# One batch of attention over each MLP, a pipelined head, and squares and value casts on GpSimd, in a fused attention and mixer kernel

## The chip, the cores and the metric

One core of one Trainium2 chip (trn2). The time is that of the device for one execution, in microseconds. Most executions of one kernel agree within 0.3%. Every run was timed beside the kernel before on the same chip, and results were compared with the reference. An execution is called slow here when it took over 1.5% longer than the fastest of the same kernel.

## The reference, cut to what matters

```python
batch, n_heads, seq, head_dim = 8, 12, 448, 64        # d_model = 768, rank = 32
def attn(q, k, v, g_q, g_k):                           # q, k, v: [8, 12, 448, 64] float32
    q_n, k_n = rmsnorm(q, g_q), rmsnorm(k, g_k)        # over head_dim, eps 1e-6
    scores = q_n @ k_n.T / sqrt(64)
    return softmax(scores) @ v
def mixer(x, U, V, w_ch1, w_ch2):                      # x: [8, 448, 768], from attn
    u = x + (x.T @ U @ V).T                            # low-rank mix along seq
    return u + relu(u @ w_ch1) @ w_ch2                 # 768 -> 3072 -> 768
```

The MLP has the most arithmetic. Attention needs TensorE too, but also ScalarE (exponentials) and VectorE (norms, copies out of PSUM, divisions), so both kernels weave pieces of attention between pieces of an MLP.

## The kernel before

Words used throughout: a *tile* `t` is four heads of one batch (three tiles per batch), loaded together. A *pair* `p` is two heads, half a tile (six pairs per batch). Per pair TensorE makes 8 transposes (to `pt`), 8 score matmuls (to `sc`) and 32 value matmuls (to `o`). `pt` and `o` share one PSUM buffer, the pool `ps_o`. The *head* is everything up to the first matmul of the first MLP (`ph`); *after the head* is the rest. One MLP has 24 groups of `ph` matmuls, then the `po` matmuls. An even batch uses 384 columns and an odd one 512, because a seventh of every even batch (64 of its 448 columns) is carried into the odd one.

The parts that the change and the argument touch, with cuts marked:

```python
def setup():                                  # (cut)
    for half in range(2):
        nc.scalar.dma_start(gg[...], g_q...); nc.scalar.dma_start(gk2[...], g_k...)
    nc.vector.tensor_mul(gg, gg, gk2)         # first work of VectorE: waits for g
def setup_mix():
    nc.gpsimd.memset(Uf, 0.0)
    for ...:                                  # 14 small loads
        nc.scalar.dma_start(Uf[...], Ur[j, p0:p1, :])
    nc.vector.tensor_copy(Ub, Uf)
    for i in range(4):
        nc.scalar.dma_start(Vf[...], moe_V)
    nc.vector.tensor_copy(V4..., Vf...)       # (cut)
def load(t):                                  # SyncE's queue, qk has 2 buffers
    nc.sync.dma_start(qk[:, 0], q[...]); nc.sync.dma_start(qk[:, 1], k[...])
def load_v(t):                                # GpSimd's queue; the DMA casts to bf16
    for h in range(HG):
        nc.gpsimd.dma_start(va[:, h, :, 0:D], v[b, h0 + h]...)
def stats(t):
    for s in range(2):
        nc.scalar.activation(sq[:, s], qk[:, s], AF.Square)
        nc.vector.tensor_reduce(rstd[:, s]..., sq[:, s]..., AX, OP.add)
    nc.scalar.activation(rs, rs, AF.Ln, bias=eps); nc.scalar.activation(rs, rs, AF.Exp, scale=-0.5)
def scale(t):                                 # four tensor_tensor: qkn = qk * rstd
    ...
def transposes(p):                            # pt from ps_o, then
    nc.vector.tensor_scalar(qT, pt[:, 0], gg, None, OP.mult); nc.vector.tensor_copy(kT, pt[:, 1])
def values(p, hh):                            # o from ps_o, then three VectorE operations
    ...
def attention(b):                             # order within a pair
    for p in range(b * 6, b * 6 + 6):         # scores(p, (0, 1)), expo(p, 0)
        ...                                   # values(p - 1, 0); expo(p, 1)
        ...                                   # even pair: stats(t + 1)
        ...                                   # scores(p, (2, 3)), expo(p, 2)
        ...                                   # values(p - 1, 1); expo(p, 3)
        ...                                   # odd pair: scale(t + 1), load(t + 3)
        ...                                   # transposes(p + 1)
# the order of work
attention(0) ; setup_mix() in the middle of it
for b in range(B):
    if b == 0:
        for _, piece in first[:6] + mixing(0): piece()      # first = attention(1)
        weave(fill, 24 * 384, first[6:])                    # 11 pairs over the first MLP
        weave(fill, total - 24 * 384 - 3000, attention(2))
    else:
        weave(fill, total * 0.84, attention(b + 2) or the last two values)
    weave(fill, total * 0.13, mixing(b + 1))
```

## Time and profile before

| | before |
|---|---|
| time, median of 4 | 719.97 us (719.29 to 720.61) |
| span in the profile | 719.2 us |
| head (up to the first `ph` matmul) | 89.25 us |
| after the head | 629.97 us |
| TensorE idle in the head / after it | 50.95 / 34.03 us |

Idle times in these tables are sums of the gaps in front of TensorE's matmuls in the trace. From the page of the kernel before: the share of time in which TensorE was busy, then its busy tenths in 40 slices of 18 us, and the clock that it was granted:

```profile
PE 629.4 (88%) x5168; PEld 357.1 (50%) x5168; DVE 342.7 (48%) x773; ACT 272.0 (38%) x385; POOL 80.4 (11%) x126
...
PE   1606787878899999989999999989999999999997
...
PEclk9999799989999999999999999999999999999999
```

The kernel is bound by TensorE, with a slow head. By stretch (columns: the stretch, its length, busy time and count for each engine, the granted clock, the share of the DMA engines and GB/s); these are the head, the first three MLPs with what is woven into them, and the last MLP, which carries nothing:

```profile
core 0: us, PE busy (x) PEld busy (x) DVE busy (x) ACT busy (x) POOL busy (x), PEclk, DMA share, GB/s
0.00:89.25 89.25, 38.20 (x342) 23.02 (x343) 38.86 (x92) 36.62 (x48) 29.75 (x54) 0.94 1.05 169
89.25:199.70 110.45, 89.02 (x868) 51.40 (x869) 64.51 (x153) 55.85 (x77) 15.47 (x22) 0.95 0.50 85
199.70:284.80 85.10, 83.38 (x675) 45.63 (x673) 45.11 (x101) 34.31 (x48) 8.45 (x12) 1.00 0.33 60
284.80:356.70 71.90, 68.38 (x623) 40.53 (x621) 40.06 (x92) 32.92 (x48) 8.44 (x12) 1.00 0.36 65
650.30:719.20 68.90, 64.06 (x349) 33.73 (x346) 13.66 (x22) 7.17 (x12) 0.00 (x0) 1.00 0.10 29
```

TensorE is busy for 38 of the 89 us of the head. The first MLP, which carries 11 pairs, takes 110 us and leaves 21 us idle. Its even successor, with six pairs, takes 72 us. The busy time of the last line stops short of 68.9 us because the last store is in it.

Why the head is slow shows in the timeline (start, length, engine, line, operation, output and input, count; in brackets the idle time of the engine before it and what ended it):

```profile
10.80 0.16 DVE L100 TENSOR_TENSOR gg<-gg,gk_93 128x1 f32<-128x1 f32 x1 [10.80 <-DMA gk_93<-in_g_k_dram]
10.88 2.34 DVE L155 TENSOR_REDUCE rstd<-sq 112x16 f32<-112x1024 f32 x2
...
39.09 9.06 ACTq L112 DMA_DIRECT2D Uf<-in_moe_U_dram  x13
...
51.37 0.29 DVE L113 CAST Ub<-Uf 128x256 bf16<-128x256 f32 x1 [12.53 <-DMA Vf<-in_moe_V_dram]
...
54.62 0.99 PE L194 MATMUL sc<-qT,kT 64*112 64x448 bf16 x4 [14.79 <-DVE kT L185]
...
57.61 1.06 PE L215 MATMUL o<-va_98,E_95 112*128 112x65 bf16 x16
```

The first reduce stands behind the gain multiply, and that waits for `g` until 10.8 us, although the first squares were done at 5.9 us. Then 14 loads of U and 4 of V leave ScalarE's queue for 12.7 us. VectorE's copy of U stands in front of the copies of the next transposes, so TensorE waits 14.79 us. The last line gives 1.06 us for 16 value matmuls. Later in the trace the same group takes 0.67 us:

```profile
94.33 0.67 PE L215 MATMUL o<-va_97,E_95 112*128 112x65 bf16 x16
```

Eight transposes take 1.16 us in the head and 0.57 us later. So TensorE runs the head at about half speed. The row PEclk reads 9 there because the trace's clock records begin only at 74.4 us; the durations show it.

What TensorE waited for after the head (who, for whom: us in all, times, longest):

```profile
PE sc L194 <- DVE kT L185: 13.3, 19, 1.5
...
PE pt L180 <- DVE xs_100 L222: 6.7, 5, 2.1
PE pt L180 <- DVE qkn L168: 6.6, 16, 1.4
...
PE pt L180 <- DVE xs_101 L222: 4.5, 3, 1.9
```

Scores wait for the copy of `kT` out of PSUM, and transposes for `qkn`, the output of `scale`, and for `ps_o` to be evicted. All of it is VectorE's work, and 21.5 of the 34 us are in the first MLP. Squares and `scale` on the same page (busy us, mean ns, then the idle before them):

```profile
L168 DVE TENSOR_TENSOR qkn<-qk,rstd 112x512 bf16<-112x512 f32 x96 | 59.7, 682 | 1.0 <-ACT rstd L159 0.7
...
L154 ACT ACTIVATE sq<-qk 112x1024 f32<-112x1024 f32 x48 | 48.2, 1058 | 4.0 <-DMA qk<-in_q_dram 2.9
```

### The profile page before, as it was taken

How to read it: one execution, taken by the hardware profiler on the slowest of the kernel's cores; microseconds unless marked ns; L12 is line 12 of the kernel's file. 1: busy time of each engine (PE TensorE's matmuls, PEld its weight loads, DVE VectorE, ACT ScalarE, POOL GpSimd, SP SyncE). 2: the span in 40 equal slices, each digit the busy share in tenths (PEclk: the TensorE clock that was granted, in tenths of full speed). 3: DMA queues.
4: the chain of work that ended last, by engine and by line, in shares of the span. 5: the costliest groups of instructions: out<-in, count | busy, mean ns of one | idle time of the engine just before them, and what ended most of it. 6: DMA issues, size and time to landing. Idle time of an engine off the chain costs nothing.

```text
span 719.2 us, 12074 instructions
## 1 busy us (share of the span) xinstructions
PE 629.4 (88%) x5168; PEld 357.1 (50%) x5168; DVE 342.7 (48%) x773; ACT 272.0 (38%) x385; POOL 80.4 (11%) x126
## 2 busy tenths in 40 slices
PE   1606787878899999989999999989999999999997
PEld 0303444444454565555554556555544656664464
DVE  3425655656555545645556544654555333233211
ACT  2615455555354530664165322554255211101200
POOL 7203111112001010111010110111000000000000
PEclk9999799989999999999999999999999999999999
DMA  9995993345413333234413423324300010010011
GB/s 143 221 174 83 224 147 59 49 71 102 83 29 62 48 69 92 20 62 86 100 11 62 83 43 89 62 18 88 94 5 1 23 46 22 1 46 22 1 45 44
DMA packets 80854, 49.09 MB, mean 68 GB/s; under 512 B 47905, under 2 KB 77217, under 8 KB 80801
## 3 DMA queue, kind: packets, MB, share of 16 engines
q0 software_dynamic: 52416, 14.95, 20.4%
q1 hardware_dynamic: 26752, 33.04, 17.2%
q8 instruction: 40, 0.66, 0.4%
q10 hardware_dynamic: 1632, 0.35, 0.3%
q14 instruction: 14, 0.11, 0.1%
HBM read 52.25 MB, written 11.01 MB: 88 GB/s over the span
## 4 chain that ended last, share of the span: by engine, by line
PE 71%; DVE 17%; ACT 5%; DMA 4%; issue 2%; ACTq 0%; SPq 0%; DVEq 0%
PE po L296 28%; PE ph L276 24%; DVE qkn L168 7%; PE sc L194 6%; PE o L215 6%; DVE rstd L155 5%; ACT E_95 L199 2%; PE pt L180 2%; DMA qk<-in_k_dram 2%; ACT sq L154 2%; DVE qT L184 1%; PE pu L256 1%; PE pu L253 1%; PE po L294 1%; DMA gk_93<-in_g_k_dram 1%
## 5 line engine op out<-in xcount | busy, mean ns | idle before, releaser
L296 PE MATMUL po<-w2b,hT 128*128 128x384 bf16 x1344 | 246.1, 328 | 0.0
L296 PEld LDWEIGHTS <-hT 128*128 128x128 bf16 x1344 | 125.8, 98 | 81.9 <-issue 9.5
L276 PEld LDWEIGHTS <-w1b 128*128 128x128 bf16 x1152 | 104.8, 98 | 99.6 <-issue 14.1
L279 ACT ACTIVATE hT<-ph 128x384 bf16<-128x384 f32 (+1 forms) x96 | 52.2, 544 | 230.8 <-PE ph L276 230.6
L276 PE MATMUL ph<-uB,w1b 128*128 128x512 bf16 x576 | 133.4, 379 | 0.0
L199 ACT ACTIVATE E_95<-sc 112x896 bf16<-112x896 f32 x96 | 84.8, 911 | 78.2 <-PE sc L194 66.2
L281 DVE TENSOR_SCALAR hT<-ph 128x384 bf16<-128x384 f32 (+1 forms) x96 | 59.8, 623 | 101.1 <-PE ph L276 100.7
L199 ACT ACTIVATE E_96<-sc 112x896 bf16<-112x896 f32 x96 | 84.8, 914 | 51.8 <-PE sc L194 51.8
L276 PE MATMUL ph<-uA,w1b 128*128 128x384 bf16 x576 | 104.0, 326 | 0.1
L194 PE MATMUL sc<-qT,kT 64*112 64x448 bf16 x384 | 66.0, 410 | 40.3 <-DVE kT L185 34.3
L218 DVE RECIPROCAL rec<-o 128x4 f32<-128x4 f32 x96 | 17.3, 180 | 109.2 <-PE o L215 109.2
L180 PE MATMUL pt<-ident,qkn 112*128 112x112 bf16 x384 | 31.5, 224 | 42.1 <-DVE qkn L168 25.7
L155 DVE TENSOR_REDUCE rstd<-sq 112x16 f32<-112x1024 f32 x48 | 56.3, 1213 | 22.2 <-ACT sq L154 21.9
L168 DVE TENSOR_TENSOR qkn<-qk,rstd 112x512 bf16<-112x512 f32 x96 | 59.7, 682 | 1.0 <-ACT rstd L159 0.7
L194 PEld LDWEIGHTS <-kT 64*112 64x112 bf16 x384 | 21.9, 134 | 74.9 <-DVE kT L185 50.2
L180 PEld LDWEIGHTS <-qkn 112*128 112x128 bf16 x384 | 23.1, 102 | 56.8 <-DVE qkn L168 32.4
L154 ACT ACTIVATE sq<-qk 112x1024 f32<-112x1024 f32 x48 | 48.2, 1058 | 4.0 <-DMA qk<-in_q_dram 2.9
L147 POOL DMA_DIRECT2D va_99<-in_v_dram x32 | 22.5, 704 | 177.2 <-PE o L215 170.8
L215 PEld LDWEIGHTS <-E_95 112*128 112x128 bf16 x768 | 33.1, 103 | 10.4 <-issue 3.2
L215 PEld LDWEIGHTS <-E_96 112*128 112x128 bf16 x768 | 32.7, 103 | 10.8 <-issue 3.6
L147 POOL DMA_DIRECT2D va_98<-in_v_dram x32 | 22.5, 704 | 134.4 <-PE o L215 134.4
L147 POOL DMA_DIRECT2D va_97<-in_v_dram x32 | 22.6, 708 | 132.4 <-PE o L215 128.6
(99 smaller groups left out, 370.6 us busy)
## 6 DMA issues: line engine op xcount, KB each, us to landing
qk<-in_q_dram SPq DMA_DIRECT2D x24, 448.0 KB, 4.1
qk<-in_k_dram SPq DMA_DIRECT2D x24, 448.0 KB, 5.5
w1b<-in_moe_w_ch_dram POOLq DMA_DIRECT2D x6, 768.0 KB, 17.8
w2b<-in_moe_w_ch_dram POOLq DMA_DIRECT2D x6, 768.0 KB, 17.2
out_dram<-osb SPq DMA_DIRECT2D x8, 336.0 KB, 2.8
out_dram<-osb SPq DMA_DIRECT2D x8, 288.0 KB, 2.7
out_dram<-osb SPq DMA_DIRECT2D x8, 240.0 KB, 2.6
va_97<-in_v_dram POOLq DMA_DIRECT2D x32, 56.0 KB, 2.6
```

The costliest lines, as they stand in the source:

```text
L147: nc.gpsimd.dma_start(va[:, h, :, 0:D], v[b, h0 + h].rearrange("(p j) d -> p j d", j=NJ))
L154: nc.scalar.activation(sq[:, s], qk[:, s], AF.Square)
L155: nc.vector.tensor_reduce(rstd[:, s].rearrange("p h j -> p (h j)"), sq[:, s].rearrange("p h (j d) -> p (h j) d", d=D), AX, OP.add)
L168: nc.vector.tensor_tensor(qkn[:, pr, s].rearrange("p j h d -> p h j d"), qk[:, s, hp].rearrange("p h (j d) -> p h j d", d=D), rstd[:, s, h ...
L180: nc.tensor.transpose(pt[:, s, j * SP:(j + 1) * SP], qkn[:, p % 2, s, j].rearrange("p h d -> p (h d)"), ident[:SP, :SP])
L194: nc.tensor.matmul(sc[:, hh, 0:S], kT[pp, kc * SP:(kc + 1) * SP], qT[pp, :], start=True, stop=True)
L199: nc.scalar.activation(Es[p % NE][:, :, PAD + kc * S:PAD + (kc + 1) * S], scs.pop((p, kc))[:, :, 0:S], AF.Exp, scale=float(D) ** 0.5)
L215: nc.tensor.matmul(o[:, i, :], E[:, hh, c:c + P], va[:, hl, kc, :], start=(kc == 0), stop=(kc == NJ - 1))
L276: nc.tensor.matmul(ph, w1b[:, dc, hc * P:(hc + 1) * P], u[:, dc, :], start=(dc == 0), stop=(dc == KD - 1))
L279: nc.scalar.activation(hT[:, hc, 0:n], ph, AF.Relu)
L281: nc.vector.tensor_relu(hT[:, hc, 0:n], ph)
L296: nc.tensor.matmul(po, hT[:, hc, i * P:(i + 1) * P], w2b[:, hc, hs], start=False, stop=(hc == KH - 1))
```

## The change

The intent: attention is always one batch ahead and spread evenly over the whole MLP; the head is a software pipeline by pairs; squares and the casts of the values move to GpSimd; TensorE is kept warm by 30 matmuls on zeros at the start. The core of the diff, cuts marked with `...`:

```diff
-    xpool = ctx.enter_context(tc.tile_pool(name="xpool", bufs=3))
+    xpool = ctx.enter_context(tc.tile_pool(name="xpool", bufs=2))
-    NE, NV = 2, 3
+    NE, NV, NWARM, NFILL = 2, 3, 30, 0
...
-                    nc.scalar.dma_start(Uf[r:r + p1 - p0, par, i, :], Ur[j, p0:p1, :])
+                    nc.sync.dma_start(Uf[r:r + p1 - p0, par, i, :], Ur[j, p0:p1, :])
...  (loads of U and V in load_mix, called early; the copies in setup_mix, called later)
     def load_v(t):
-        for h in range(HG):
-            nc.gpsimd.dma_start(va[:, h, :, 0:D], v[b, h0 + h].rearrange("(p j) d -> p j d", j=NJ))
+        vt = loads.tile([SP, HG, NJ * D], FP32, tag="vt")
+        nc.sync.dma_start(vt, v[b, h0:h0 + HG].rearrange("h (p j) d -> p h (j d)", j=NJ))
+    def cast_v(t):
+        nc.gpsimd.tensor_copy(vas[t % NV][:, :, :, 0:D], vts.pop(t)...)
+    def squares(t):
+        for s in range(2):
+            if t < 2:
+                nc.scalar.activation(sqs[t, s], qks[t][:, s], AF.Square)
+            else:
+                nc.gpsimd.tensor_tensor(sqs[t, s], qks[t][:, s], qks[t][:, s], OP.mult)
...  (stats is split in squares, reduce and rsqrt; scale in two halves)
-    def attention(b):
+    def attention(b, head=False):
         for p in range(b * 6, b * 6 + 6):
+            add(1, scores, p, (0, 1)); add(0, expo, p, 0)
+            if p + 1 < NP:
+                add(1, transposes, p + 1)           # was the last piece of the pair
+            if odd and t + 2 < NT:
+                add(0, reduce, t + 2)               # was one tile ahead, now two
+            add(1, expo, p, 1)
+            if p % 6:
+                add(1, values, p - 1, 0)
+            if not odd:
+                ... scale(t + 1, 0)                 # was at the end of the odd pair
+                ... squares(t + 2)
+            add(1, scores, p, (2, 3)); add(0, expo, p, 2)
+            if odd and t + 2 < NT:
+                add(0, rsqrt, t + 2)
+            if p % 6:
+                add(1, values, p - 1, 1)
+            if ...:                                 # even pair
+                add(0, scale, t + 1, 1); add(0, cast_v, t + 1)
+            if odd and t + 3 < NT:
+                add(0, load, t + 3); add(0, load_v, t + 3)
+            add(1, expo, p, 3)
+            ...                                     # head: setup_mix, w1 loads
+        add(1, values, b * 6 + 5, 0); add(1, values, b * 6 + 5, 1)
...
+        heat(NWARM)
...  (the gain multiply comes after the first scale)
         for b in range(B):
             fill, total = mlp(b), volume(b % 2)
-            ...  (as above: 11 pairs over the first MLP, then two batches ahead)
             if b + 1 < B:
-                weave(fill, total * 0.13, mixing(b + 1))
+                weave(fill, total * 0.86, attention(b + 1))
+                weave(fill, total * 0.11, mixing(b + 1))
```

More of the change, by code (lines that the diff above doesn't have):

```diff
@@ L96, in setup @@
             nc.gpsimd.memset(t, 0.0)
+        nc.gpsimd.memset(Uf, 0.0)
+        nc.gpsimd.memset(Vsh, 0.0)
         for half in range(2):
@@ L99, in setup, with load_mix @@
             nc.scalar.dma_start(gk2[half * D:(half + 1) * D, :], g_k.rearrange("(d o) -> d o", o=1))
-        nc.vector.tensor_mul(gg, gg, gk2)
-    def setup_mix():
-        Uf = consts.tile([P, 2, 4, rank], FP32, name="Uf")
-        Vf = consts.tile([P, S], FP32, name="Vf")
-        nc.gpsimd.memset(Uf, 0.0)
+    Uf = consts.tile([P, 2, 4, rank], FP32, name="Uf")
+    Vf = consts.tile([P, S], FP32, name="Vf")
+    def load_mix():
         Ur = moe_U.rearrange("(p j) r -> j p r", j=NJ)
@@ L111, in setup_mix @@
                     r += lo - off
-                    nc.scalar.dma_start(Uf[r:r + p1 - p0, par, i, :], Ur[j, p0:p1, :])
+                    nc.sync.dma_start(Uf[r:r + p1 - p0, par, i, :], Ur[j, p0:p1, :])
+        for i in range(4):
+            nc.sync.dma_start(Vf[i * rank:(i + 1) * rank, :], moe_V)
+    def setup_mix():
         nc.vector.tensor_copy(Ub, Uf)
-        for i in range(4):
-            nc.scalar.dma_start(Vf[i * rank:(i + 1) * rank, :], moe_V)
         nc.vector.tensor_copy(V4.rearrange("r (j p) -> r j p", j=NJ), Vf.rearrange("r (p j) -> r j p", j=NJ))
-        nc.gpsimd.memset(Vsh, 0.0)
         nc.vector.tensor_copy(Vsh[:, 0, 0:64], V4[:, 384:448])
@@ L133 @@
     NT, NP = B * 3, B * 6
-    qks, rstds, qkns, qTs, scs, x3_of = {}, {}, {}, {}, {}, {}
+    qks, vts, sqs, rstds, qkns, qTs, scs, x3_of = {}, {}, {}, {}, {}, {}, {}, {}
     def load(t):
@@ L144, in load_v @@
         b, h0 = t // 3, (t % 3) * HG
-        va = vas[t % NV]
-        for h in range(HG):
-            nc.gpsimd.dma_start(va[:, h, :, 0:D], v[b, h0 + h].rearrange("(p j) d -> p j d", j=NJ))
-    def stats(t):
-        qk = qks[t]
-        sq = norm.tile([SP, 2, HG, NJ * D], FP32, tag="sq", bufs=1)
-        rstd = norm.tile([SP, 2, HG, NJ], FP32, tag="rstd")
-        for s in range(2):
-            nc.scalar.activation(sq[:, s], qk[:, s], AF.Square)
-            nc.vector.tensor_reduce(rstd[:, s].rearrange("p h j -> p (h j)"),
-                                    sq[:, s].rearrange("p h (j d) -> p (h j) d", d=D), AX, OP.add)
-        rs = rstd.rearrange("p s h j -> p (s h j)")
+        vt = loads.tile([SP, HG, NJ * D], FP32, tag="vt")
@@ new lines, in load_v @@
+        nc.sync.dma_start(vt, v[b, h0:h0 + HG].rearrange("h (p j) d -> p h (j d)", j=NJ))
+        vts[t] = vt
+    def cast_v(t):
+        nc.gpsimd.tensor_copy(vas[t % NV][:, :, :, 0:D], vts.pop(t).rearrange("p h (j d) -> p h j d", d=D))
+    def squares(t):
+        for s in range(2):
+            sqs[t, s] = norm.tile([SP, HG, NJ * D], FP32, tag="sq", name="sq")
+            if t < 2:
+                nc.scalar.activation(sqs[t, s], qks[t][:, s], AF.Square)
+            else:
+                nc.gpsimd.tensor_tensor(sqs[t, s], qks[t][:, s], qks[t][:, s], OP.mult)
@@ L158, in stats, with reduce, rsqrt @@
+    def reduce(t):
+        rstds[t] = norm.tile([SP, 2, HG, NJ], FP32, tag="rstd", name="rstd", bufs=3)
+        for s in range(2):
+            nc.vector.tensor_reduce(rstds[t][:, s].rearrange("p h j -> p (h j)"),
+                                    sqs.pop((t, s)).rearrange("p h (j d) -> p (h j) d", d=D), AX, OP.add)
+    def rsqrt(t):
+        rs = rstds[t].rearrange("p s h j -> p (s h j)")
         nc.scalar.activation(rs, rs, AF.Ln, bias=eps)
         nc.scalar.activation(rs, rs, AF.Exp, scale=-0.5)
-        rstds[t] = rstd
@@ L162, in scale @@
-    def scale(t):
-        qk, rstd = qks.pop(t), rstds.pop(t)
-        qkn = norm.tile([SP, 2, 2, NJ, 2, D], BF16, tag="qkn")
-        for pr in range(2):
-            hp = slice(2 * pr, 2 * pr + 2)
-            for s in range(2):
-                nc.vector.tensor_tensor(
-                    qkn[:, pr, s].rearrange("p j h d -> p h j d"),
-                    qk[:, s, hp].rearrange("p h (j d) -> p h j d", d=D),
-                    rstd[:, s, hp].rearrange("p h j -> p h j ()").to_broadcast([SP, 2, NJ, D]),
-                    OP.mult)
-        qkns[t] = qkn
+    def scale(t, pr):
+        qk, rstd = qks[t], rstds[t]
+        if pr == 0:
+            qkns[t] = norm.tile([SP, 2, 2, NJ, 2, D], BF16, tag="qkn", name="qkn")
+        hp = slice(2 * pr, 2 * pr + 2)
+        for s in range(2):
+            nc.vector.tensor_tensor(
+                qkns[t][:, pr, s].rearrange("p j h d -> p h j d"),
+                qk[:, s, hp].rearrange("p h (j d) -> p h j d", d=D),
+                rstd[:, s, hp].rearrange("p h j -> p h j ()").to_broadcast([SP, 2, NJ, D]),
+                OP.mult)
@@ L307, in mlp, with add @@
                 yield HALF
-    def attention(b):
+    def attention(b, head=False):
         items = []
+        def add(weight, fn, *args):
+            items.append((weight, lambda: fn(*args)))
         for p in range(b * 6, b * 6 + 6):
             t, odd = divmod(p, 2)
-            def start(p=p, t=t, odd=odd):
-                if not odd and 2 < t + 1 < NT:
-                    load_v(t + 1)
-                scores(p, (0, 1))
-                expo(p, 0)
-            items.append((1, start))
-            if p > 0:
-                items.append((1, lambda p=p: values(p - 1, 0)))
-            items.append((1, lambda p=p: expo(p, 1)))
-            if not odd and t + 1 < NT:
-                items.append((0.5, lambda t=t: stats(t + 1)))
-            items.append((1, lambda p=p: (scores(p, (2, 3)), expo(p, 2))))
-            if p > 0:
-                items.append((1, lambda p=p: values(p - 1, 1)))
-            items.append((1, lambda p=p: expo(p, 3)))
-            if odd and t + 1 < NT:
-                items.append((1, lambda t=t: scale(t + 1)))
-                if t + 3 < NT:
-                    items.append((0, lambda t=t: load(t + 3)))
-            if p + 1 < NP:
-                items.append((1, lambda p=p: transposes(p + 1)))
@@ new lines, in attention @@
+            late = head and p == 0
+            add(1, scores, p, (0, 1))
+            add(0, expo, p, 0)
+            if head and p == 1:
+                add(0, scale, 1, 0)
+            if p + 1 < NP:
+                add(1, transposes, p + 1)
+            if odd and t + 2 < NT:
+                add(0, reduce, t + 2)
+            if late:
+                add(0, reduce, 1)
+            add(1, expo, p, 1)
+            if p % 6:
+                add(1, values, p - 1, 0)
+            if not odd:
+                if t + 1 < NT and not late:
+                    add(0, scale, t + 1, 0)
+                if t + 2 < NT:
+                    add(0, squares, t + 2)
@@ new lines, in attention @@
+            add(1, scores, p, (2, 3))
+            add(0, expo, p, 2)
+            if odd and t + 2 < NT:
+                add(0, rsqrt, t + 2)
+            if p % 6:
+                add(1, values, p - 1, 1)
+            if t + 1 < NT and (p == 1 if head and t == 0 else not odd):
+                add(0, scale, t + 1, 1)
+                add(0, cast_v, t + 1)
+            if odd and t + 3 < NT:
+                add(0, load, t + 3)
+                add(0, load_v, t + 3)
+            add(1, expo, p, 3)
@@ L336, in attention @@
+            if late:
+                add(0, rsqrt, 1)
+            if head and p == 2:
+                add(0, setup_mix)
+            if head and p in (0, 2, 3):
+                for i in range((0, 0, 2, 4)[p], (2, 0, 4, 6)[p]):
+                    add(0, load_w1, i)
+        add(1, values, b * 6 + 5, 0)
+        add(1, values, b * 6 + 5, 1)
         return items
@@ L351, in weave, with heat @@
             piece()
-    def finish_batch(b):
-        return [(1, lambda: values(b * 6 + 5, 0)), (1, lambda: values(b * 6 + 5, 1))]
+    def heat(n):
+        if n:
+            warm = ps_mm.tile([P, 512], FP32, tag="mm")
+            for _ in range(n):
+                nc.tensor.matmul(warm, xss[1][:, 0:P], xss[1][:, 0:512], start=True, stop=True)
     def volume(par):
@@ L360 @@
     with tc.manual_schedule():
-        for t in range(2):
-            load(t)
+        load(0)
+        load(1)
+        load_v(0)
+        load_v(1)
         setup()
-        for t in range(3):
-            load_v(t)
-        stats(0)
-        scale(0)
+        heat(NWARM)
+        squares(0)
+        reduce(0)
+        rsqrt(0)
+        scale(0, 0)
+        nc.vector.tensor_mul(gg, gg, gk2)
+        transposes(0)
+        squares(1)
+        scale(0, 1)
         load(2)
-        for i in range(3):
-            load_w1(i)
-        transposes(0)
-        for i, (_, piece) in enumerate(attention(0)):
+        load_v(2)
+        load_mix()
+        cast_v(0)
+        for _, piece in attention(0, head=True):
             piece()
-            if i == 20:
-                setup_mix()
-                for i in range(3, 6):
-                    load_w1(i)
+        for _, piece in mixing(0):
+            piece()
+        for i in range(6):
+            load_w2(i)
         for b in range(B):
             fill, total = mlp(b), volume(b % 2)
-            if b == 0:
-                first = attention(1)
-                for _, piece in first[:6] + mixing(0):
-                    piece()
-                for i in range(6):
-                    load_w2(i)
-                weave(fill, 24 * 384, first[6:])
-                weave(fill, total - 24 * 384 - 3000, attention(2))
-            else:
-                att = attention(b + 2) if b + 2 < B else []
-                if b + 2 == B:
-                    att = finish_batch(B - 1)
-                weave(fill, total * 0.84, att or [(1, lambda: None)])
             if b + 1 < B:
-                weave(fill, total * 0.13, mixing(b + 1))
+                weave(fill, total * 0.86, attention(b + 1))
+                weave(fill, total * 0.11, mixing(b + 1))
             for _ in fill:
```

## The prediction

> **What bounds the kernel now.** TensorE, after a slow head. In the page's engine table PE is busy 629 of 719 us (88%), VectorE 48%, ScalarE 38%, GpSimd 11%. By time (timeline):
> - Head, 0 to 89 us: attention of batch 0, one pair of batch 1, first mixing. PE idles 51 us: 14.7 until the first transposes (the first reduce queues behind the gain multiply, which waits for g until 10.8), 14.8 in one wait from 39 to 54 us (18 small U/V loads leave ScalarE's queue, and the copies that need them block VectorE), the rest on VectorE. A pair takes about 8 us. PE is at half speed: 16 value matmuls take 1.06 us, later 0.67. The clock row reads 9 there; the durations disagree.
> - 89 to 192 us: the first MLP carries 11 pairs; PE idles 21.5 us, and the clock drops to 0.5 for three stretches of 3.4 us.
> - 192 to 587 us: PE idles 12 us, 1.5 (odd) to 3.7 (even) per batch. After 587: 0.2 us.
>
> **Work PE cannot shed** (start-to-start spacing, timeline): an MLP matmul costs 216 ns at 512 columns, 163 at 384: 48 us for an even and 64 for an odd batch, 447 us in all; a woven pair 2.7 us; a mixing 3 us; tail 5 us.
>
> **The change** puts one batch of attention over each of MLPs 0 to 6. After the head: 447 + 7x(3 + 6x2.7) + 5 = 586 us plus stalls; before, that stretch lasted 630 us. The overfull first MLP loses most of its idle time and its cold windows. Squares leave ScalarE (24x2.0 us) for GpSimd, about two tiles early; 96 casting value loads become 24 plain loads and GpSimd casts. Neither was on the chain after 192 us. GpSimd's cost, estimated from the Trainium skill, "GPSIMD Engine Reference", section 3.1 (4497 ns for 2048 fp32): 2.2 us per square, 5.5 per tile with the cast, against a tile period over 20 us. No run here shows it yet. I allow 12 us of stalls for the steady part.
>
> **Head.** First scores at 13 us instead of 17; no U/V wait. Pair 0 about 4 us, then about 6.8 per pair, bound by the single ps_o buffer passing from PE to VectorE and back three times a pair, with PE mostly cold again after the warm-up matmuls. Pairs 1 and 3 are late by 3 to 8 us: reduce waits for GpSimd squares, which wait for loads that wait for a buffer. Last values and mixing 8 to 10 us. First MLP matmul at 66 to 72 us, against 89.
>
> **Sum.** 70 + 586 + 12 = 668 us, range 650 to 688. Faster by over 2%: 0.96; within 2%: 0.03; slower: 0.01.
>
> **What would show each step.** First scores near 13 us; no gap near 39; first MLP matmul at 66 to 72; 16 value matmuls near 1.06 us in mid-head; PE idle after the head below 20 us; MLPs 0, 2, 4, 6 about 70 us each, 1, 3, 5 about 85; ScalarE busy down by 45 us, GpSimd near 130, VectorE unchanged.
>
> **What would make it wrong.** (a) The Trainium skill, "SBUF — State Buffer", "two separate sides", calls the port pair shared by VectorE and GpSimd an exclusive lock, which a VectorE instruction with two SBUF inputs contends for: scale (0.68 us now) may wait behind squares and stall evictions, up to 20 us more. Scale's mean time would show it. (b) w1 and w2 are issued behind GpSimd squares: w2, landed by 98 us now, may come after po wants it (about 103 us): 5 to 10 us. (c) The head stays warm: 8 us less. (d) Squares slower than 2.2 us lengthen the head.

## The result, and the profile after

A ratio is the mean time of one kernel's fast runs over the mean of the other's fast runs of the same rounds, so it is not quite the ratio of the medians that are quoted. All outputs are right.

| | before | after | difference |
|---|---|---|---|
| time, median of 4 | 719.97 us | 657.36 us (656.28 to 657.83) | ratio 0.913 (0.911 to 0.914) |
| span in the profile | 719.2 us | 655.2 us | -64.0 |
| head | 89.25 us | 67.27 us | -22.0 |
| after the head | 629.97 us | 587.96 us | -42.0 |
| TensorE idle in the head / after it | 50.95 / 34.03 us | 26.08 / 0.96 us | |

The same parts of the page after the change:

```profile
PE 623.4 (95%) x5198; PEld 355.5 (54%) x5198; DVE 346.3 (53%) x773; ACT 231.0 (35%) x341; POOL 120.8 (18%) x98
...
PE   6556999999999999999999999999999999999997
...
PEclk9566999999999999999999999999999999999999
```

And the same stretches: head, the first three MLPs, and the last.

```profile
core 0: us, PE busy (x) PEld busy (x) DVE busy (x) ACT busy (x) POOL busy (x), PEclk, DMA share, GB/s
0.00:67.27 67.27, 41.06 (x365) 23.48 (x365) 42.72 (x92) 28.49 (x39) 31.16 (x41) 0.70 0.99 201
67.27:135.10 67.83, 67.58 (x621) 40.49 (x622) 42.93 (x95) 27.44 (x42) 17.56 (x11) 1.00 0.64 141
135.10:218.10 83.00, 83.00 (x675) 45.61 (x673) 43.08 (x100) 28.82 (x42) 14.22 (x9) 1.00 0.27 70
218.10:285.80 67.70, 67.45 (x624) 40.47 (x622) 41.67 (x94) 27.44 (x42) 14.26 (x9) 1.00 0.33 80
586.40:655.20 68.80, 64.03 (x349) 33.74 (x346) 13.63 (x22) 7.16 (x12) 0.00 (x0) 1.00 0.11 29
```

The two heads do not hold quite the same work: that of before also has the scores and exponentials of one pair of batch 1 (8 score matmuls), which the changed kernel does after the head.

After the head TensorE is busy without a hole: 67.6 of 67.8 us and 83.0 of 83.0 us. The first MLP is now an ordinary one. In the head the granted clock is 0.70 on average, which here includes records from 7 us on.

The timeline of the new head, at the places that answer to those shown of before:

```profile
13.22 0.59 PE L204 MATMUL sc<-qT,kT 64*112 64x448 bf16 x4 [0.84 <-DVE kT L195]
...
19.17 2.99 DVE L179 TENSOR_TENSOR qkn<-qk,rstd 112x512 bf16<-112x512 f32 x2 [0.65 <-ACT rstd L171]
19.59 4.32 POOL L160 TENSOR_TENSOR sq<-qk 112x1024 f32<-112x1024 f32 x2 [5.68 <-DMA qk<-in_q_dram]
...
29.53 0.33 SPq L141 DMA_DIRECT2D qk<-in_q_dram  x1
...
38.34 3.74 POOL L160 TENSOR_TENSOR sq<-qk 112x1024 f32<-112x1024 f32 x2 [11.61 <-DMA qk<-in_q_dram]
...
43.99 1.06 PE L225 MATMUL o<-va_98,E_95 112*128 112x65 bf16 x16 [4.65 <-DVE xs_100 L232]
```

The first scores start at 13.2 us instead of 17.1, and there is no gap at 39 us. Two `scale` operations take 2.99 us together, over twice their usual time, while GpSimd squares (second and third line): the first took 0.69 us, the second 2.38 us. The load of tile 3 is issued at 29.5 us, its squares start at 38.3 us when it lands, and the value matmuls of pair 3 wait 4.65 us at 44 us, because the eviction before them stands behind the reduce of tile 3 on VectorE. The end of the head:

```profile
61.21 1.06 PE L225 MATMUL o<-va_99,E_96 112*128 112x65 bf16 x16 [0.79 <-DVE xs_100 L232]
...
67.27 1.29 PE L286 MATMUL ph<-uA,w1b 128*128 128x384 bf16 x6
```

Sixteen value matmuls still take 1.06 us at 61 us: the warm-up did not last. GpSimd's squares and VectorE's `scale` on the page:

```profile
L160 POOL TENSOR_TENSOR sq<-qk 112x1024 f32<-112x1024 f32 x44 | 83.2, 1907 | 381.9 <-DVE rstd L165 188.8
...
L179 DVE TENSOR_TENSOR qkn<-qk,rstd 112x512 bf16<-112x512 f32 x96 | 66.6, 734 | 1.8 <-ACT rstd L171 1.4
```

### The profile page after: what moved, and what is told of

Same layout as the page of the kernel before. It is cut to its first block, busy times and chain, and to the rows that moved or that the text cites. A ratio compares the mean times of both kernels' runs of the same rounds, so it can differ in the third digit from the quotient of the medians.

```text
span 655.2 us, 12039 instructions
## 1 busy us (share of the span) xinstructions
PE 623.4 (95%) x5198; PEld 355.5 (54%) x5198; DVE 346.3 (53%) x773; ACT 231.0 (35%) x341; POOL 120.8 (18%) x98
## 4 chain that ended last, share of the span: by engine, by line
PE 89%; DVE 3%; ACT 2%; DMA 1%; POOL 1%; issue 0%; POOLq 0%
PE po L306 34%; PE ph L286 33%; PE o L225 8%; PE sc L204 7%; PE pt L190 3%; PE pu L263 2%; PE pu L266 2%; ACT E_95 L209 1%; DMA qk<-in_q_dram 1%; PE po L304 1%; DVE rstd L165 1%; DVE qkn L179 1%; ACT hT L289 1%; PE pm L250 1%; POOL sq L160 1%
## 5 line engine op out<-in xcount | busy, mean ns | idle before, releaser
L160 POOL TENSOR_TENSOR sq<-qk 112x1024 f32<-112x1024 f32 x44 | 83.2, 1907 | 381.9 <-DVE rstd L165 188.8
L209 ACT ACTIVATE E_96<-sc 112x896 bf16<-112x896 f32 x96 | 86.2, 911 | 80.4 <-PE sc L204 80.3
L209 ACT ACTIVATE E_95<-sc 112x896 bf16<-112x896 f32 x96 | 85.4, 912 | 60.2 <-PE sc L204 60.2
L179 DVE TENSOR_TENSOR qkn<-qk,rstd 112x512 bf16<-112x512 f32 x96 | 66.6, 734 | 1.8 <-ACT rstd L171 1.4
L204 PE MATMUL sc<-qT,kT 64*112 64x448 bf16 x384 | 63.2, 394 | 2.9 <-ACT E_95 L209 1.2
L194 DVE TENSOR_SCALAR qT<-pt,gg 128x448 bf16<-128x448 bf16 x48 | 21.5, 448 | 46.7 <-PE pt L190 46.6
L225 PEld LDWEIGHTS <-E_95 112*128 112x128 bf16 x768 | 32.1, 101 | 20.1 <-DVE xs_100 L232 8.6
L225 PEld LDWEIGHTS <-E_96 112*128 112x128 bf16 x768 | 32.3, 102 | 12.2 <-DVE xs_100 L232 3.9
L190 PE MATMUL pt<-ident,qkn 112*128 112x112 bf16 x384 | 28.5, 218 | 5.9 <-DVE qkn L179 4.8
L272 DVE CAST uB<-pu 128x448 bf16<-128x448 f32 x24 | 14.5, 620 | 8.6 <-PE pu L266 8.6
L195 DVE COPY kT<-pt 128x448 bf16<-128x448 bf16 x48 | 18.3, 381 | 0.0
```

What stands on the lines that cost most here:

```text
L160: nc.gpsimd.tensor_tensor(sqs[t, s], qks[t][:, s], qks[t][:, s], OP.mult)
L179: nc.vector.tensor_tensor(qkns[t][:, pr, s].rearrange("p j h d -> p h j d"), qk[:, s, hp].rearrange("p h (j d) -> p h j d", d=D), rstd[:, ...
L190: nc.tensor.transpose(pt[:, s, j * SP:(j + 1) * SP], qkn[:, p % 2, s, j].rearrange("p h d -> p (h d)"), ident[:SP, :SP])
L204: nc.tensor.matmul(sc[:, hh, 0:S], kT[pp, kc * SP:(kc + 1) * SP], qT[pp, :], start=True, stop=True)
L209: nc.scalar.activation(Es[p % NE][:, :, PAD + kc * S:PAD + (kc + 1) * S], scs.pop((p, kc))[:, :, 0:S], AF.Exp, scale=float(D) ** 0.5)
L225: nc.tensor.matmul(o[:, i, :], E[:, hh, c:c + P], va[:, hl, kc, :], start=(kc == 0), stop=(kc == NJ - 1))
```

## The experiments

Twelve runs were made, of eleven kernels. The changed kernel's ratio to the kernel before is 0.913. Medians and ratios (95% intervals), all to the kernel before of the same rounds:

| run | what it is | median us | ratio | head, after the head us |
|---|---|---|---|---|
| head_waits | before, two waits of the head removed | 703.56 | 0.976 (0.974 to 0.978) | see the repeat |
| head_waits_again | the same, one run | 702.08 | - | 71.5, 628.7 |
| placement | before, one batch over each MLP | 706.26 | 0.981 (0.979 to 0.983) | 88.2, 616.2 |
| two_ahead | after, with the old placement | 669.45 | 0.929 (0.927 to 0.931) | 67.2, 600.8 |
| no_warm | after, without warm-up | 656.91 | 0.912 (0.910 to 0.913) | 67.4, 588.0 |
| sq_act_steady | after, squares on ScalarE after the head | 662.38 | 0.919 (0.918 to 0.921) | 67.5, 593.4 |
| cast_dma | after, casting value loads | 657.30 | 0.913 (0.911 to 0.914) | 67.2, 588.1 |
| late_transposes | after, transposes last in a pair | 657.28 | 0.912 (0.911 to 0.913) | 67.6, 587.7 |
| late_scale | the same, and scale right before them | 668.70 | 0.929 (0.927 to 0.931) | 68.3, 598.9 |
| head_early | after, another head, first try | 668.43 | 0.928 (0.927 to 0.929) | 78.5, 588.0 |
| head_order | second try | 659.35 | 0.916 (0.914 to 0.918) | see below |
| head_last | third try | 651.70 | 0.905 (0.903 to 0.907) | 62.9, 588.0 |

The medians are over all executions, in head_waits and head_order one slow one among four included; the ratios use the fast ones. The traces of sq_act_steady, cast_dma, late_transposes and head_early lack 21 of the 5198 matmul records, and each missing record leaves a small gap that counts as idle. In cast_dma and head_early, which have no gap over 0.15 us after the head, the sum is 2.3 us for this reason, against 0.96 in the changed kernel. Sums of idle for these four are therefore about 1.4 us too large.

### Two waits of the head

The kernel before, with the loads of U and V early on SyncE's queue and the gain multiply after the first `scale`:

```diff
-        nc.vector.tensor_mul(gg, gg, gk2)            # in setup
...
-                    nc.scalar.dma_start(Uf[...], Ur[j, p0:p1, :])
+                    nc.sync.dma_start(Uf[...], Ur[j, p0:p1, :])     # in load_mix; V likewise
...
         scale(0)
+        nc.vector.tensor_mul(gg, gg, gk2)
         load(2)
+        load_mix()
```

> The kernel before with two waits of its head removed and nothing else: the U and V loads leave SyncE's queue early instead of ScalarE's in the middle, and the gain multiply comes after the first scale. Theory (the 14.8 us wait at 39 us and the late first reduce are on the chain): about 17 to 19 us less, 701 to 704 us, and the stretch after the first MLP matmul stays at 630 us. Rival (the head is bound by weight loads or VectorE work, so a removed wait only uncovers the next): less than 8 us gained, 712 us or more.

Measured: 703.56 us, ratio 0.976; the fast runs are 702.62 to 704.05 us. The profiled execution alone took 2671 us (see the last section), so the kernel ran once more for a trace.

> The same kernel as head_waits, for a trace, because the profiled run of the first was a 2670 us outlier. 702 to 704 us; first scores near 13 us, no 14.8 us wait at 39 us, first MLP matmul at 71 to 74 us, PE idle after it 34 us and the first MLP's clock dips as before.

Measured: 702.08 us in the single run. First scores at 13.4 us, first `ph` at 71.5 us, 34.3 us of idle after it; only two stretches at clock 0.5 fell in the first MLP instead of three. The theory stands: the two waits were worth 17.8 us of the head (89.25 less 71.47), and the time after it changed by only 1.3 us (629.97 against 628.67). The two were removed together; their shares were not measured apart.

### Placement and order, crossed

The kernel before with the new placement only: the rest of the next batch's attention and the two last values of it over one MLP.

```diff
-                weave(fill, 24 * 384, first[6:])
-                weave(fill, total - 24 * 384 - 3000, attention(2))
-            else: ...
+            if b + 1 < B:
+                nxt = attention(b + 2) if b + 2 < B else finish_batch(B - 1)
+                weave(fill, total * 0.84, first[6:] + nxt[:6])
+                first = nxt
+                weave(fill, total * 0.13, mixing(b + 1))
```

> The kernel before with only the placement changed: six pairs over each of the MLPs 0 to 6, in the old order within a pair, squares on ScalarE, casting value loads. Theory (the overfull first MLP causes 20 of the 34 us idle, even spreading alone leaves 1.5 to 3.7 us of idle per batch): about 700 us, head unchanged with the first MLP matmul near 89 us, PE idle after it 15 to 20 us. Rival 1 (the order within a pair removed the idle, not the placement): 714 us or more. Rival 2 (placement does it all): below 690 us with under 3 us idle after the head.

Measured: 706.26 us, ratio 0.981. The head is unchanged (88.2 us); the idle after it is 20.1 us, as the theory had it, but four stretches of 3.4 us at clock 0.5 remain, and the total is 6 us over the expected 700. Idle is now alike from MLP to MLP, 2.5 us in an odd and 3.6 us in an even batch (1.7 us in the seventh MLP). What TensorE waits for after the head in that run:

```profile
PE sc L194 <- DVE kT L185: 13.1, 17, 1.5
...
PE pt L180 <- DVE qkn L168: 5.2, 18, 0.4
```

The reverse: the changed kernel with the old placement.

```diff
-                weave(fill, total * 0.86, attention(b + 1))
-                weave(fill, total * 0.11, mixing(b + 1))
+            if b == 0:
+                weave(fill, 24 * 384, attention(1))
+                weave(fill, total - 24 * 384 - 3000, attention(2))
+            elif b + 2 < B:
+                weave(fill, total * 0.84, attention(b + 2))
...  (mixing at 0.13; xpool 3 and opool 2 buffers)
```

> The changed kernel with the old placement: attention of batches 1 and 2 over the first MLP, then two batches ahead; everything else as changed (one output buffer less, so that the third x buffer fits). Theory (both placement and order count, VectorE needs some 75 of 80 us in that MLP): 8 to 15 us more than the changed kernel, 665 to 672 us, nearly all of it idle inside the first MLP. Rival 1 (order alone suffices): within 4 us of 657. Rival 2 (placement alone counts): 677 us or more.

Measured: 669.45 us, ratio 0.929, with 10.8 us of idle in the first MLP and 1.1 us in the rest. The first MLP in that run:

```profile
67.20:163.60 96.40, 85.77 (x908) 50.38 (x909) 71.71 (x161) 49.56 (x72) 32.08 (x20) 1.00 0.63 142
```

Twelve pairs over one MLP keep VectorE busy for 71.7 of 96.4 us, and that is not full; still value matmuls wait for its evictions (6.3 us on `xs`, 2.7 us on `kT`). So the placement is worth 13.8 us in the old order (629.97 less 616.22) and 12.9 us in the new one (600.85 less 587.96): it adds to the rest of the change and hardly depends on it. (The buffer less of `opool` costs at most about 1 us here: the odd MLPs take 83.4 instead of 83.0 us.)

### The warm-up

```diff
-    NE, NV, NWARM, NFILL = 2, 3, 30, 0
+    NE, NV, NWARM, NFILL = 2, 3, 0, 0
```

> The changed kernel without its 30 warm-up matmuls. Theory (the clock falls back to 0.5 at 17.5 us anyway, and in the head PE waits for VectorE): 0 to 2 us more, so 657 to 659 us. Rival (TensorE kept warm is what speeds the head): 5 us or more.

Measured: 656.91 us, ratio 0.912 against 0.913: no difference that the intervals can tell. The first transposes and scores are slow without it (8 transposes 1.16 us instead of 0.56), and the first `ph` comes at 67.4 us instead of 67.3. In the changed kernel the clock falls back to 0.5 at 17.5 us. The head then waits for VectorE and for loads, whatever TensorE's clock.

### Squares on ScalarE after the head

```diff
-            if t < 2:
+            if t < 2 or t >= 5:
                 nc.scalar.activation(sqs[t, s], qks[t][:, s], AF.Square)
```

> The changed kernel with the squares of tiles 5 to 23 back on ScalarE, at the same place in the program; the head keeps them on GpSimd. Theory (after the head the squares are off the chain; ScalarE is busy 203 of 588 us there and has room for 38 us more): 656 to 661 us, GpSimd busy down by 72 us, PE idle after the head below 4 us. Rival (ScalarE's 2 us squares delay exponentials and so the scores, as the change assumes): 667 us or more, with waits of scores on ScalarE.

Measured: 662.38 us, ratio 0.919: 0.7% slower than the changed kernel, between theory and rival and a little above the theory's range. GpSimd's busy time is down by 70 us; the idle after the head sums to 7.0 us instead of 1.0, of which about 1.4 us are missing records; the stretch after the head is 5.4 us longer (593.37 against 587.96). What TensorE waits for after the head:

```profile
PE sc L204 <- ACT E L209: 4.8, 9, 0.8
```

My "off the chain" was wrong in this order of work. ScalarE is busy for only 33 of 69 us in an even MLP, but in its program the squares stand in front of exponentials that scores wait for, 4.8 us in all. Moving them to GpSimd is worth about 5 us, not nothing, and not 10.

### Casting value loads

```diff
-        vt = loads.tile(...); nc.sync.dma_start(vt, v[...])          # in load_v
-        nc.gpsimd.tensor_copy(vas[t % NV][:, :, :, 0:D], vts.pop(t)...)  # in cast_v
+        for h in range(HG):
+            nc.gpsimd.dma_start(vas[t % NV][:, h, :, 0:D], v[b, h0 + h]...)
```

> The changed kernel with values again loaded by casting DMAs from GpSimd's queue, issued where the cast stood. Theory (value loads are off the chain after the head; in the head their 128-byte writes take longer on the DMA engines): 657 to 663 us, PE idle after the head unchanged near 1 us. Rival (they cost time throughout, as the change assumes): 667 us or more, with value matmuls waiting for va.

Measured: 657.30 us, ratio 0.913, the same as the changed kernel, with GpSimd busy for 163.5 us instead of 120.8. The value loads are off the chain, in the head too, although the casting ones do cost the DMA engines more: 43008 packets of 128 bytes took 1378 us of their time in this trace, and the plain loads, in packets of 1024 bytes, some 767 us in that of the changed kernel (the difference of SyncE's queue between the two).

### Where the old order lost its time

```diff
-            if p + 1 < NP:
-                add(1, transposes, p + 1)
+            if p + 1 < NP and head: ...
...
             add(1, expo, p, 3)
+            if p + 1 < NP and not head:
+                add(1, transposes, p + 1)
```

> The changed kernel with the transposes of the next pair, after the head, again at the end of a pair instead of behind its first scores. Theory (issuing them early is what removed the wait of scores on the kT copy, 1.3 to 2.2 us per batch in the old order): 7 to 15 us of idle in the seven batches, scores waiting for the kT copy, 664 to 672 us. Rival (early scale, reduce and squares removed the idle, not the transposes): within 3 us of 657.

Measured: 657.28 us, ratio 0.912: nothing changed, and the theory fell. Idle after the head sums to 3.7 us, about 1.4 us of it missing records, and the seven MLPs take as long as before within 1.1 us each. The theory that took its place is that `scale`, not the transposes, has to be early. So `scale` went back as well, in one block right before the transposes:

```diff
+            if odd and not head and t + 1 < NT:
+                add(0, scale, t + 1, 0)
+                add(0, scale, t + 1, 1)
...  (the two early halves only in the head; transposes last, as above)
```

> The changed kernel with, after the head, scale of the next tile in one block at the end of the odd pair and the transposes right behind it, as in the order before; squares stay on GpSimd, reduce stays early. Late transposes alone changed nothing. Theory now (scale just ahead of its transposes is what made scores wait for the kT copy and transposes for qkn, 2.5 to 3.6 us idle per batch with the placement alone): idle after the head 10 to 20 us, 667 to 677 us. Rival (squares off ScalarE, with the statistics done a tile earlier, removed the idle): within 4 us of 657.

Measured: 668.70 us, ratio 0.929, idle after the head 11.3 us. What TensorE waits for after the head:

```profile
PE sc L204 <- DVE kT L195: 7.6, 11, 1.1
...
PE o L225 <- DVE kT L195: 2.8, 3, 0.9
```

So this theory stands. Four `scale` operations of 0.68 us in one block put 2.7 us of VectorE's work in front of the `kT` copy that the next scores wait for, and the block returns 11 us. An even MLP goes from 67.7 to 70.4 us and an odd one from 83.0 to 83.2 us.

### A better head, in three tries

The wait of 4.65 us at 44 us pointed to the load of tile 3, which waits for a buffer that the second half of `scale` of tile 1 frees. First try: that half earlier, the load right behind it, squares of tiles 2 to 4 on ScalarE.

```diff
             if head and p == 1:
                 add(0, scale, 1, 0)
+                add(0, scale, 1, 1); add(0, load, 3); add(0, load_v, 3)
...
+            if head and p == 1:
+                add(0, squares, 2); add(0, reduce, 2)
...
-            if t < 2:
+            if t < 5:
```

> A better head, tried: both halves of scale of tile 1 together and the load of tile 3 right behind, squares of tiles 2 to 4 on ScalarE, which idles there. Theory (pair 3 waits 5.4 us because the load of tile 3 waits for its buffer until 29.5 us and then shares the DMA engines with w1, and squares on GpSimd take twice as long and block scale by up to 1.7 us): first MLP matmul at 59 to 63 us instead of 67.3, total 649 to 653 us. Rival (DMA transfers bound the head; w1, now issued from 14 us on, delays the loads of tiles 2 and 3): no gain, 656 us or more.

Measured: 668.43 us, ratio 0.928: 11 us slower. The theory fell, though not quite to its rival. The timeline:

```profile
17.77 15.18 SPq L113 DMA_DIRECT2D Uf<-in_moe_U_dram  x14
...
35.89 0.36 SPq L141 DMA_DIRECT2D qk<-in_q_dram  x1
...
44.38 1.06 ACT L158 ACTIVATE sq<-qk 112x1024 f32<-112x1024 f32 x1 [10.11 <-DMA qk<-in_q_dram]
...
50.31 0.62 PE L204 MATMUL sc<-qT,kT 64*112 64x448 bf16 x2 [12.76 <-ACT E L209]
```

The 14 loads of U take 15.2 us to leave SyncE's queue, and the load of tile 3 stands behind them and those of V: issued at 35.9 us, its q part landed at 44.4 us and its k part at 48.4 us. The squares on ScalarE wait for it in front of exponentials, and TensorE waits 12.76 us. Second try: U and V behind the load of tile 3, and w1 behind the value casts of tiles 1 and 2.

```diff
                 add(0, load, 3); add(0, load_v, 3)
+                add(0, load_mix)
...
+            if late:                              # pair 0
+                add(0, cast_v, 1); add(0, cast_v, 2)     # in front of load_w1(0), (1)
-            if head and p == 2:
+            if head and p == 4:
                 add(0, setup_mix)
```

> A second try at the head, as the first with these differences: the U and V loads follow the load of tile 3 instead of holding SyncE's queue for 12 us ahead of it, and w1 waits behind the value casts of tiles 1 and 2, so that the load of tile 2 has the DMA engines to itself. Theory (the first try failed because the load of tile 3 was issued at 36 us behind U/V, and ScalarE's exponentials then stood behind squares that waited for it 12.8 us): tile 3 issued by 23 us and landed by 32, no wait over 3 us in the head, first MLP matmul at 60 to 64 us, total 649 to 653 us. Rival (with w1 in flight the loads come too late whatever the order): 656 us or more.

Measured: 659.35 us, ratio 0.916; the fast runs are 658.73 to 659.52 us. Only the profiled execution was slow (810 us, with a granted clock of 0.75 or 0.5), so its stretch after the head is not used; the head runs at the low clock anyway in all these kernels. In it the load of tile 3 was issued at 23.5 us and landed at 29.4, as expected. But the load of tile 4 was issued at 39.2 us behind U and V and landed at 51.7, with all of w1 and most of w2 in flight, and 8.5 us of waits of scores on ScalarE took its place. That was the rival's reading, so the third try put the tile loads ahead of the weights:

```diff
-            if t < 5:
+            if t < 4:                             # squares of tile 4 on GpSimd again
...  (load_mix behind the load of tile 4; setup_mix in pair 5)
-            if head and p in (0, 2, 3):           # w1 parts 2 to 5 in pairs 2 and 3
+            if head and p == 4:                   # behind those squares; w2 follows
+                for i in range(2, 6):
                     add(0, load_w1, i)
```

> A third try at the head: as the second, but the tile loads go ahead of the weights: only w1 parts 0 and 1 are issued early, parts 2 to 5 behind the GpSimd squares of tile 4, w2 behind them, and U/V behind the load of tile 4. Theory (in the second try the wait only moved from tile 3 to tile 4, whose load was issued at 39 us behind U/V and shared the DMA engines with all of w1 and w2): load of tile 4 landed by 42 us, no wait over 4 us in the head, first MLP matmul at 60 to 64 us, total 650 to 654 us. Rival (the weights must pass in the same time, so the wait moves on to the first MLP, for w2 or for tile 5): 656 us or more, with idle inside the first MLP.

Measured: 651.70 us (651.21 to 653.58), ratio 0.905 (0.903 to 0.907), against 0.913 of the changed kernel: 0.9% faster, and the fastest of all. The first `ph` comes at 62.9 us. The loads of tile 4 (first line) and of w1 parts 2 to 5 in that run, and the squares that stand between:

```profile
35.27 0.31 SPq L141 DMA_DIRECT2D qk<-in_q_dram  x1
...
41.62 3.88 POOL L160 TENSOR_TENSOR sq<-qk 112x1024 f32<-112x1024 f32 x2 [15.66 <-DMA qk<-in_q_dram]
...
46.90 3.35 POOL L128 DMA_DIRECT2D w1b<-in_moe_w_ch_dram  x4
```

The load of tile 4 landed at 43.5 us, slightly later than the 42 that was expected; no wait of the head after the first transposes is over 2 us; and the first MLP has 0.4 us of idle, so that the last part of w2, landing at 100.7 us, was not missed, although `po` began at 96.4 us. The rival fell. This try moved squares, half a `scale`, loads and the copies of U and V together, so its 0.9% is not split among them.

## Why the prediction was right, point by point

The measured 657.4 us lies 10.6 us under the predicted 668 and inside the range; the mechanism was right in the main and two terms of the sum were too large. (The terms add up to the span, 655.2 us, and the time is 2 us longer.)

- **Head, "first MLP matmul at 66 to 72 us", entered as 70.** 67.3 us. First scores at 13.2 us, no gap at 39 us, pairs 1 and 3 late, with TensorE waiting for VectorE between the three uses of `ps_o`: all as predicted. From first scores to first scores pairs 0 to 4 took 3.6, 10.7, 6.3, 11.2 and 5.6 us. The two waits removed alone gave 17.8 of the 22.0 us; the other 4.2 were not tested apart, and the score matmuls that left the head are in them.
- **"586 us plus stalls" after the head.** Without its 0.96 us of idle it took 587.0 us. The durations from the trace of before, 216 and 163 ns per matmul and 2.7 us per pair, held.
- **"I allow 12 us of stalls for the steady part".** This is the mis-sized term: 0.96 us was measured. I took over the old order's idle per batch (1.5 to 3.7 us) as if it belonged to the placement. It belonged to the order: with the new placement and the old order 20.1 us of idle remain. Moving `scale` back returns 10.4 us of idle (11.3 less 1.0), and squares back on ScalarE 5.4 us of time (its idle sum is too large by the missing records). These two sum to 16 of the 19 us of idle between the placement run and the changed kernel; they were not run together. MLP by MLP the account fits less well. In the even batches the two runs return 13.9 us of time, more than the 11.6 us of idle that the placement run has over the changed kernel there; in the odd ones they return 2.5 of 7.6 us. So some 5 us of idle in the odd batches have no tested cause. That the sums of squares are reduced a tile earlier than before was in no run taken back alone. Early transposes alone and value loads contribute nothing.
- **"The overfull first MLP loses most of its idle time and its cold windows."** Right: 21.5 us of idle became 0.4, and no clock record under 1 remains until the end. Placement as a whole is worth 13 to 14 us, shown from both sides.
- **"Neither was on the chain after 192 us"** (squares and value loads). Right of the chain before and right of the value loads, but it misled me about squares: in the new order they would cost 5 us on ScalarE.
- **"PE mostly cold again after the warm-up matmuls"**, 16 value matmuls near 1.06 us. Right for 9 of the 12 groups of the head; the others, near or inside the short warm stretches, took 0.82 to 1.04. Without the warm-up the time is the same.
- **Engines.** ScalarE's busy time fell by 41 us (45 predicted), GpSimd's is 120.8 (130), VectorE's rose by 3.6 ("unchanged").
- **(a) The port lock.** The trace agrees with the Trainium skill, "SBUF — State Buffer", section "SBUF: two separate sides", that the two block each other: the longest `scale` took 2.38 us against 0.69 before. Each of the six `scale` operations that took over 0.75 us began under a GpSimd operation and ended 0.54 to 0.56 us after that one ended; three times it was a square and three times a cast of the values. But these are only 6 of 96 operations, at 5.0 us of VectorE's time in all, 1.2 us of it after the head. The feared 20 us did not come.
- **(b) w2 late.** It landed at 94.5 us and `po` began at 100.8 us: it did not happen, with 6 us to spare.
- **(d) Slow squares.** One took 1.89 us in the median, under the estimate of 2.2 us.

Of the 42 us gained after the head, the placement run gives 13.8. The other 28.3 us split into 19.2 us of idle (20.1 less 0.96) and about 6.4 us for four stretches at half clock (the same MLP takes 73.1 us with one and 71.5 without). Some 2.7 us stay unattributed.

## What to carry to other kernels

When two kinds of work are woven on one engine, count the waits of the woven work per order, not per unit of work: a block of 2.7 us on a helper engine just ahead of the copy that the main engine needs cost 11 us, and splitting it and issuing it one pair earlier made it free. Even spreading and a good order add up, so test them apart and together. An engine with half of its time free can still delay another, if work that the other waits for stands behind its other work; and in a head that fills the DMA engines, the order of the loads counts (the first and second try, 668.4 and 659.4 us, differ in the order of loads and of the casts and copies that go with them): move those that gate the next piece ahead of bulk weights, and keep long trains of small loads out of their queue.

## What the Trainium skill lacked or had wrong

- "TensorE: Matmul & The Clock Gate", Part 1, has the clock fall after an idle window of about 3.4 us, and the page's closing table advises no idle gaps over about 3 us. Its section on a second failure mode tells of falls through frequent short idle times, but gives no busy share. Here the clock fell after windows of 3.4 us in which TensorE was not idle: busy for 0.48, 0.33 and 0.29 of the window (changed kernel, windows starting at 14.0, 34.5 and 51.6 us, union of the matmuls' spans), with no single gap in the first over 0.82 us. It stayed up after windows of 0.53 to 0.59 (before, 98 to 133 us). It did not rise after windows busy for 0.71 to 0.76, and rose after those busy for 0.93 to 1.00. No sharp threshold follows: in two_ahead it fell after a window of 0.55, and in head_waits_again it rose after one of 0.84. These windows were laid by the clock records' own times; that the hardware uses just this measure is not shown.
- The same page, in its caveat on clock records, tells of a clock stuck at a quarter for over 50 us. One execution here (head_waits, 2669 us) was slow for its whole length: `ph` matmuls came 840 and 630 ns apart in the last five MLPs (216 and 163 normally), 3.9 times as long, and 1047 to 1279 ns apart in the first three. Its trace has no clock record at all, and so its mean clock reads 1.0. Another execution (head_order, 810 us) had records of 0.75 before 20 us and from 67 us on, and 0.5 between, in a program of one core; `ph` matmuls came 266 and 212 ns apart. Both were single executions of kernels whose other runs were normal, and their cause is open.
- "GPSIMD Engine Reference", section 3.1, gives a two-input operation of 2048 fp32 as 4497 ns. Half the size with both inputs the same tile took 1892 ns here, less than half of that; a one-input cast of 1024 fp32 to bf16 took 1038 ns, which the page does not list.
- No page that I found says that the profile's clock row reads as full speed before the first clock record (74.4 us in the kernel before), where 16 value matmuls took 1.06 us instead of 0.67.
